# A fused attention and matrix-product kernel: whole loads of two first tiles, and the small products of tiles 3 to 5 placed in other bursts

## The chip, the core and the metric

The kernel runs on one core of a Trainium2 chip. Five engines work from queues of their own: TensorE (PE, with its weight loads as PEld), VectorE (DVE), ScalarE (ACT), GpSimd (POOL) and SyncE (SP), which here only issues the DMAs. The metric is the device time of one execution in microseconds, median of three. The profile is of one further execution.

## What is computed

```python
def sm_attn(qq, kk, vv):                 # per batch (8) and head (8), head_dim 64
    s = scale * qq @ kk.T
    a = exp(s - max(s));  a = a / (sum(a) + 1e-9)
    return a @ vv
p_packed = sm_attn(p, k, v)              # 32 packed queries over 576 keys
out      = sm_attn(q, p_packed, p_packed) # 576 queries over the 32 packed ones
x = out as (4608 tokens, 512)
h = max(x @ w1, x @ w2, x @ w3)          # 768 wide
result = h @ w_out
```

## The kernel before

A batch is 576 tokens, worked in two halves of 288 columns. Heads are packed four to a tile: `r` (0, 1) is the parity of a head in its pair. Per batch PE does, in the program's names:

- `s1`: the first scores (`scores`, stage S), 16 small products of 64 rows by 32 columns of the array (form 64*32). Their softmax weights `a1` come from DVE (maximum) and ACT (exponential), stage A.
- `spread` (stage X): DVE transposes `a1` in blocks into `x`, one DMA writes it to DRAM (`xk`), four DMAs read it back turned (`xt`).
- `av` (`values`, stage V): 40 products of `xt` with `v`, then (stage K) a transpose, which gives `pt`, the packed values.
- `s2` (`queries`, stage Q): the second scores, 16 products of 64*32, and their softmax (stage B), which gives `a2h` and `a2l`, high and low part.
- `pw` (`project`, stage P): for each of six tiles j of the 768 hidden features, 8 products of `pt` with the weights `w`, 64*32. ACT and DVE read them out of PSUM into `ph` and `pl`.
- `mi` (`layer_in`, stage N): 216 full products (128*128, 288 columns), in groups of six: one group is one tile j, one half, one of w1 to w3. A group's sum stands in a PSUM buffer of the pool `moe`, which has 4; it is free for the next group when ACT or DVE has taken it out (`maximum`, stage E).
- `mo` (`layer_out`, stage O): 126 full products with w_out, read out in stage F.

Small products stand in bursts between the full ones, since they use the array in another shape. PSUM has a second pool, `big`, with 2 buffers, for `s1`, `av`, `s2` and the tiles of `pw` that `project` doesn't put into `moe`.

The order of everything is written out by hand: START (batches 0 and 1 and the conversion of the weights), then LOOP once for each batch b = 2 to 7. Each word is one step of a stage; `P03` is tile 3 of batch b, `P10` tile 0 of batch b+1, `V101` is `av` of batch b+1, `Q1` its `s2`, `X1` its spread. A letter v, g or a behind a word says which engine does the step. Each engine runs its part of that order in the order in which it stands; it only waits for what an instruction needs. DMAs are issued by SP in the same way. Each DMA issue takes one of eight completion counters in turn, so it also waits until the DMA eight before it has landed. `J` words are products of no use that fill time at the start.

Of the kernel before, what the change touches and what calls it, by code (L numbers as in the profile page):

```python
# [20 lines left out]
B, H, S, D, NP = 8, 8, 576, 64, 32  # L21
# [24 lines left out]


START = """
k00 k01 J10 S0 A01 A01 J7 A01 A00 A00 v01 w00 C00 q010 v00 q000 A01 A00 A00v C00 C00 J1 V00 Z00 q001 V00 V01 Z01
V01 J1 K0 w01 K0v C01 J1 Q0 B010 B010 q011 J1 Q0 C01 k11 k10 C01 B001 B001 B000 B011 B000 B011 w02 B000v B011v  # L50
C00 k21 B010 C01 B010 B010 B000 B000 B000v J11 S1 B011 k20 w12 C02 C02 J12 S2 B001 A10 B001 C02 C02 P00 B010v
A11 A10 A11 B011 B010 B011 C12 B000 P00 B010g Z10 C12 B011 B010 w11 B010v B000g B000 v10 B001 A21 B001v P00 P00
J8 A11 Z11 B001 A20 B001g B011g B000v w10 v11 B000v A21 J1 A10 B001 q10 C12 B001v A20 C10 N00 w21 B011 B010v A10
A11 V101 C10 B011 P00 N00 V101 C11 C11 B001v C11 C12 E000 q11 N00 C21 K1 C21 w20 N00 C10 K1v J1 Q1 E000 E000 C20
C20 C21 w22 Z20 B011 N00 w30 B10 C22 C11 C10 J2 P01 P01 N00 E001 w31 B11 B11 C21 C20 C20 C22 C22 C22 w50 C30 P01
w32 B10 C31 C30 P10 w41 X2 B10v J6 N01 E010 C30 N01 C31 P02 P02 C31 w40 C32 N01 E001 E010 E001 C30 N01 N01 E011
C32 B11 C31 P02 C32 C32 E010 N02 v21 E011 N02 v20 N02 N02 w42 w52 B10 X2 H00 E020 E020 E020 B11 B11 B11v C40 C40
C40 C40 C41 C41 P03 N02 C41 P03 E021v P03 N01 N02 E021 w51 C42 C42 N03 N03 B10 X2 C41 B11 C52 B10 P10 w64 E011
C50 N03 C42 C42 E030v P10 H00 B10 Z21 N03 C52 P04 B11g P11 P04 E031 E021 E030 P04 N03 B10g w62 C52 N03 E030 N04
N04 E031 B11 C51 C51 B10 E040 E031 C52 E040 w65 H00 C50 B11 B11v P11 C51 N04 N04 B10 B10v N04 N04 E041 C64 C64  # L60
E041 E041 E040 C51 N10 C62 H02v E100 N10 N10 C50 C50 V201 q20 P11 P05 H03v w63 H02 C65 C65 C65 N11 E110 C64 C64
H03v C65 N11 N10 E100 V201 K2 E110 P05 C62 W2 N10 P05 E100 E101v C62 w60 H02v C63 N11 E110 H03v K2 q21 Q2 B21
N05 N05 C63 C63 B20 H01 E050 C63 N10 B20 B20 C60 P13 E050 W2 E101 C60 E101 P12 P13 W2 N05 H04v N05 P13 E050 C62
N11 E111 C60 N11 E111 B20 N11 W1v H03v P12 W1 P12 N13 E111 E051 N05 E051 H04 N05 N12 E051 C60 E130 N13 W1 N13
N12 W2 W2v P15 w61 C61 C61 C61 E120v E120 E130 P14 W1 W1v N13 C61 W0v W0v N12 E120 N12 W2 N13 H05g N12 W2 W2 P15
E130 H03 N12 E131 P15 B21 E121 E121 E131 P14 P14 N15 N15 N15 W0 N13 E150 E150 N14 N14 W2 N14 N14 N15 N15 E121
H03v H05 W2 W0 W0v E131 N14 W1 E150 E140 E140 E140 W0 W0 W0 H13 H04v H05 B20 E151v B20 O0 N14 E141v E141 E151
W1v N15 H01v E141 W0 k30 O0 F0 H10 O0 F0 O0 O0 O0 E151 H05v H10 W1 k31 P20 B20 H01 F0 H01v F0 W0v H10v P21 H05
B21v F0 H01 H05v P22 H01v F0 H12 H11 H14v O0 W1g H11v O0 H11v P21 B21 F0 O0 O0 H13 P20 P20 P20 H11v F0 H12 H12v
B20 O0 F0 F0 F0 F0 H13 W1v P20 O0 B20 O0 O0 H14 F0 H14v F0 F0 B21 O1 F0 H15 H15v H15 O1 H11 B21 H13v F1 F1 H15v  # L70
H15 H13v P22 O1 F1 H11v O1 H13v H15v O1 B20 F1 O1 O1 B20 O1 F1 B21 B21g P21 O1 O1 F1 F1 F1 F1 F1 F1 F1 P22 B21
O1 F1 O1 O1 F1 B21 B21 F1 O1 F1
"""


LOOP = """
S1 A10 N02 N02 N02 N02 A11 N02 E020v A10 E020 E020 N00 N00 E021v E000 Z10 X1 E021 N02 A11 P03 X1 P05 E021 H02v
P03 P04 N01 N00 v11 N00 v10 P03 P03 P03 E001 q10 N03 N03 N00 N00 H02g E000 N03 N03 N03 E030v E030 E010 N01 Z11
N03 E000 E001 E001 H00v H00 H02v E031v P04 q11 E030 H00 N01 E031 E031 P04 E010 E010 N01 N01 N01 E011 E011 E011
X1 V101 V101 H03g H03 N04 N04 N04 N04 P05 k20 K1 E041 N04 H03v N04 H01g H01v H01v K1 Q1 E040v H01 H01 H03 H03  # L80
P05 E040 E041 E040 E041 B11 B11 N05 N05 N05 N05 B10 E050 E050 H04 B10 E050 N05 B11 H04 H04 E051 E051 N05 E051
P10 B11 B10 P11 P12 H05 H05 B11 H05v P10 O0 O0 P10 O0 B10 B10 B11v H05v P12 P11 F0 B10v P10 O0 F0 H01v H03v
H05 O0 O0 F0 H05 B11 F0 P12 B10 k21 B10g O0 O0 O0 F0 P11 F0 F0 O0 B10 F0 B11g B11 F0 F0 B10g B10v P10 B11g F0
F0 O0 O0 O0 F0 F0 B11v O0 F0 F0
"""


# [1 line left out]
def fused_kernel(ctx: ExitStack, tc: tile.TileContext, kp, qt, va, vb, wi, wo, out):  # L89
# [48 lines left out]
    def doze(n):  # L138

        for i in range(0, n, 4):  # L140
            k = min(n - i, 4)
            ps = ps_moe.tile([P, 512], F32, name=f"idle{len(dozes)}", tag="moe")
            dozes.append(ps)
            nc.tensor.matmul(  # L144
                out=ps[:, 0:k * P], lhsT=ident, rhs=ident.unsqueeze(1).to_broadcast([P, k, P]),
                start=True, stop=True,
            )
# [280 lines left out]
    def project(b, j):  # L428

        parts = [slice(0, R)]  # L430
        if j == 0 and b != 1 or j == 3 and b >= 2:

            parts = [slice(r, r + 1) for r in range(R)]
            ps = [ps_moe.tile([P, 512], F32, name=f"pw{b}_{j}_{r}", tag="moe") for r in range(R)]
            src = [x[:, 0:NW * P].unsqueeze(1) for x in ps]
        else:
            x = ps_big.tile([P, R, 512], F32, name=f"pw{b}_{j}", tag="big")
            ps, src = [x[:, r] for r in range(R)], [x[:, :, 0:NW * P]]
        for n in range(4):
            for r in range(R):  # L440
                o = slice(64 * r, 64 * r + 64)
                nc.tensor.matmul(  # L442
                    out=ps[r][NP * n:NP * n + NP, 0:NW * P],
                    lhsT=pt_sb[b % 2][o, NP * n:NP * n + NP],
                    rhs=w_sb[o, j, n * NW * P:(n + 1) * NW * P],
                    start=True, stop=True,
                )
        yield 1
        hi = pool.tile([P, R, NW * P], F32R, name=f"ph{b}_{j}", tag="ph", bufs=3)
        lo = pool.tile([P, R, NW * P], F32R, name=f"pl{b}_{j}", tag="pl", bufs=3)  # L450
        pw[b, j] = (hi, lo)
        for r, x in zip(parts, src):
            nc.scalar.activation(out=hi[:, r], in_=x, func=AF.Copy, scale=2.0 ** -WS)  # L453
            yield 1
            nc.vector.scalar_tensor_tensor(  # L455
                out=lo[:, r], in0=x, scalar=2.0 ** -WS, in1=hi[:, r].bitcast(F32), op0=ALU.mult, op1=ALU.subtract,
            )
            yield 1
# [148 lines left out]
    def weigh_and_turn(b, r):  # L607
# [5 lines left out]
    stages = {  # L613
        "S": scores, "A": weigh_and_turn, "Z": invert, "X": spread, "V": lambda b, *rs: values(b, rs), "K": packed, "Q": queries,
        "B": attend, "C": convert, "P": project, "N": layer_in, "E": maximum, "H": halves,
        "O": layer_out, "F": finish, "W": weights,
    }
# [3 lines left out]
    def run(words, base):  # L621

        for word in words.split():
            name = word.rstrip("vga")
            chosen[0] = word[len(name):] or None
            kind, x = name[0], [int(i) for i in name[1:]]
            if kind == "J":
                doze(int(name[1:]))
                continue
            if kind not in "wCW":  # L630
                x[0] += base
                if x[0] >= B:
                    continue
            if kind in loads:
                loads[kind](*x)
            else:
                key = (kind, *x)
                if key not in begun:
                    begun[key] = stages[kind](*x)
                next(begun[key], None)  # L640
        chosen[0] = None

    with tc.manual_schedule():
        run(START, 0)
        for b in range(2, B):
            run(LOOP, b)


# [41 lines left out]
```

## Time and profile before

| | us |
|---|---|
| median of 3 | 468.36 (468.21 to 468.43) |
| the profiled execution | 468.03 |
| its span | 466.2 |
| PE busy | 457.3 (98%) |
| DVE, ACT, POOL busy | 349.8, 172.6, 207.1 |
| one batch of the loop, from one `s1` to the next | 54.2 |

The span is what the profiler sees from the first to the last instruction; 1.8 us of the execution's own time lie around it. PE is busy nearly always, so what counts is what PE's busy time is made of, and the few places where it waits.

### The profile page before, as it was taken

To read this page: it belongs to the slowest core of one execution; us is meant where nothing else is said; L and a number is where in the kernel's file an instruction comes from. 1 tells how busy PE (TensorE), PEld (TensorE's weight loads), DVE (VectorE), ACT (ScalarE), POOL (GpSimd) and SP (SyncE) were. 2 spreads that over 40 slices of the span, in tenths; PEclk is the share of its full clock that TensorE was granted. 3 is DMA by queue.
4 is the path that set the end of the run, shared out by engine and by line. 5 is a ranking of instruction groups with operands and counts; after the bars stand their busy time and mean duration, and the time that the engine had idled before them with its cause. 6 is when DMAs were issued, how large, how long until landed. Compare 5 with 4: busy or idle time off the path is not lost.

```text
span 466.2 us, 11503 instructions
## 1 busy us (share of the span) xinstructions
PE 457.3 (98%) x4728; PEld 405.3 (87%) x4728; DVE 349.8 (75%) x763; ACT 172.6 (37%) x333; POOL 207.1 (44%) x180
## 2 busy tenths in 40 slices
PE   8899999999999999999999999999999999999996
PEld 3456987998998998989899898989989898998996
DVE  1799989999887677766888678786777678865652
ACT  3486975744332236022340226122350324402330
POOL 0357766756332156503653055612565036531542
PEclk9999999999999999999999999999999999999999
DMA  8999883011127510193104820075101820020002
GB/s 301 403 381 312 315 296 130 1 58 56 57 73 247 192 58 1 49 308 108 59 27 141 257 100 1 27 250 188 59 1 62 296 52 1 27 76 1 2 4 99
DMA packets 25540, 59.20 MB, mean 127 GB/s; under 512 B 2448, under 2 KB 15760, under 8 KB 25488
## 3 DMA queue, kind: packets, MB, share of 16 engines
q1 hardware_dynamic: 25488, 58.47, 36.7%
q8 instruction: 37, 0.61, 0.5%
q14 instruction: 15, 0.12, 0.1%
HBM read 45.48 MB, written 12.98 MB: 125 GB/s over the span
## 4 chain that ended last, share of the span: by engine, by line
PE 92%; DVE 4%; DMA 2%; ACT 0%; issue 0%; POOL 0%; POOLq 0%; ACTq 0%
PE mi L477 49%; PE mo L546 29%; PE pw L442 7%; DMA kt<-in_kp 2%; PE s L253 2%; PE av L342 2%; PE s L370 1%; PE idle L144 1%; DVE mx L266 1%; DVE xt L219 0%; DVE w_sb L203 0%; DVE r L491 0%; ACT a L271 0%; PE tp L342 0%; DVE xl L136 0%
## 5 line engine op out<-in xcount | busy, mean ns | idle before, releaser
L477 PE MATMUL mi<-a2h,ph 128*128 128x288 f32 x576 | 173.9, 302 | 0.7 <-ACT r L131 0.5
L477 PE MATMUL mi<-a2l,ph 128*128 128x288 f32 x576 | 169.7, 295 | 0.0
L477 PE MATMUL mi<-a2h,pl 128*128 128x288 f32 x576 | 169.7, 295 | 0.0
L477 PEld LDWEIGHTS mi<-a2h,ph 128*128 128x128 f32 x576 | 108.1, 188 | 15.5 <-issue 7.1
L477 PEld LDWEIGHTS mi<-a2h,pl 128*128 128x128 f32 x576 | 108.1, 188 | 0.0
L477 PEld LDWEIGHTS mi<-a2l,ph 128*128 128x128 f32 x576 | 108.1, 188 | 0.0
L491 DVE TENSOR_TENSOR r<-mi,r 128x288 f32<-128x288 f32 x192 | 83.3, 449 | 32.6 <-PE mi L477 30.2
L131 ACT COPY r<-mi 128x288 f32<-128x288 f32 x60 | 23.4, 401 | 122.8 <-PE mi L477 122.7
L455 DVE SCALAR_TENSOR_TENSOR pl<-pw,ph 128x768 fp32r<-128x768 f32 (+1 forms) x61 | 46.8, 775 | 4.5 <-ACT ph L453 3.6
L453 ACT ACTIVATE ph<-pw 128x768 fp32r<-128x768 f32 (+1 forms) x61 | 39.9, 675 | 18.8 <-PE pw L442 15.1
L546 PE MATMUL mo<-ych,xl 128*128 128x288 f32 x144 | 42.5, 295 | 0.0
L546 PE MATMUL mo<-ych,xh 128*128 128x288 f32 x144 | 42.4, 295 | 0.0
L546 PE MATMUL mo<-ycl,xh 128*128 128x288 f32 x144 | 42.4, 294 | 0.0
L136 POOL TENSOR_TENSOR yal<-r,yah 128x576 fp32r<-128x576 f32 x13 | 18.6, 1430 | 46.1 <-ACT yah L131 46.1
L271 ACT ACTIVATE a<-s,nm 128x576 f32<-128x576 f32 x16 | 11.9, 741 | 66.8 <-DVE nm L267 60.1
L442 PE MATMUL pw<-w_sb,pt 64*32 64x384 f32 x768 | 36.0, 487 | 0.3 <-POOL w_sb L207 0.3
L207 POOL TENSOR_TENSOR w_sb<-w_sb,wi 128x512 int32<-128x512 int32 x18 | 24.2, 1349 | 26.7 <-DVE z L282 11.8
L515 POOL TENSOR_TENSOR r<-r 128x288 f32<-128x288 f32 (+1 forms) x25 | 27.9, 1128 | 17.5 <-issue 9.0
L133 POOL CAST yah<-r 128x576 fp32r<-128x576 f32 x6 | 4.0, 662 | 57.0 <-DVE r L515 57.0
L546 PE MATMUL mo<-yah,xh 128*128 128x288 f32 x96 | 28.8, 300 | 0.0
L133 DVE COPY r<-mi 128x288 f32<-128x288 f32 x36 | 16.3, 455 | 16.2 <-PE mi L477 16.2
L546 PE MATMUL mo<-ybh,xl 128*128 128x288 f32 x96 | 28.3, 295 | 0.0
(117 smaller groups left out, 885.2 us busy)
## 6 DMA issues: line engine op xcount, KB each, us to landing
kt<-in_kp SPq DMA_DIRECT2D x16, 640.0 KB, 5.2
wi<-in_wi SPq DMA_DIRECT2D x18, 512.0 KB, 6.9
v<-in_va SPq DMA_DIRECT2D x16, 512.0 KB, 5.9
q<-in_qt SPq DMA_DIRECT2D x14, 576.0 KB, 7.1
xk<-x SPq DMA_DIRECT2D x6, 576.0 KB, 4.9
wi<-in_wo SPq DMA_DIRECT2D x6, 512.0 KB, 5.0
out_t<-r SPq DMA_DIRECT2D x8, 288.0 KB, 2.2
out_t<-t SPq DMA_DIRECT2D x8, 288.0 KB, 2.3
```

Source lines behind the costliest of these rows:

```text
L131: e.copy(out=out, in_=src)
L133: e.tensor_copy(out=out, in_=src)
L136: on(default).tensor_tensor(out=lo, in0=src, in1=hi.bitcast(F32), op=ALU.subtract)
L207: nc.gpsimd.tensor_tensor(out=dst.bitcast(I32), in0=dst.bitcast(I32), in1=up, op=ALU.add)
L271: nc.scalar.activation(out=a.rearrange("p (a b) -> p a b", a=2), in_=s[:, :, 0:HS], func=AF.Exp, bias=nm, scale=SCALE, accum_out=z,)
L442: nc.tensor.matmul(out=ps[r][NP * n:NP * n + NP, 0:NW * P], lhsT=pt_sb[b % 2][o, NP * n:NP * n + NP], rhs=w_sb[o, j, n * NW * P:(n + 1) * ...
L453: nc.scalar.activation(out=hi[:, r], in_=x, func=AF.Copy, scale=2.0 ** -WS)
L455: nc.vector.scalar_tensor_tensor(out=lo[:, r], in0=x, scalar=2.0 ** -WS, in1=hi[:, r].bitcast(F32), op0=ALU.mult, op1=ALU.subtract,)
L477: nc.tensor.matmul(out=sums[b, j, hf, x][:, 0:HS], lhsT=w[:, r, x * P:(x + 1) * P], rhs=a[:, c], start=(r == 0 and n == 0), stop=(r == R - ...
L491: nc.vector.tensor_tensor(out=h, in0=sums[b, j, hf, i][:, 0:HS], in1=h, op=ALU.max)
L515: less = lambda out, x, y: on("g").tensor_tensor(out=out, in0=x, in1=y, op=ALU.subtract)
L546: nc.tensor.matmul(out=ps[:, 0:HS], lhsT=w[:, x, m * P:(m + 1) * P], rhs=h[:, z], start=(p == 0 and i == 0), stop=(p == NQ - 1 and i == 2),)
```

## The change

Two edits. In START the first batch's two `q` tiles are each loaded whole instead of in two halves; whole means 128 rows of 4608 B, a half 256 pieces of 1152 B. LOOP gets a new order for batches 2 to 5, and the old one, now called LAST, stays for batches 6 and 7. `project` puts tile 5 of batches 2 to 5 into the pool `moe` instead of `big`.

```diff
 START = """
-k00 k01 J10 S0 A01 A01 J7 A01 A00 A00 v01 w00 C00 q010 v00 q000 A01 A00 A00v C00 C00 J1 V00 Z00 q001 V00 V01 Z01
-V01 J1 K0 w01 K0v C01 J1 Q0 B010 B010 q011 J1 Q0 C01 k11 k10 ...
+k00 k01 J10 S0 A01 A01 J7 A01 A00 A00 v01 w00 C00 q01 v00 q00 A01 A00 A00v C00 C00 J1 V00 Z00 V00 V01 Z01 V01 J1
+K0 w01 K0v C01 J1 Q0 B010 B010 J1 Q0 C01 k11 k10 ...
 LOOP = """
-S1 A10 N02 N02 N02 N02 A11 N02 E020v A10 E020 E020 N00 N00 E021v E000 Z10 X1 E021 N02 A11 P03 X1 P05 E021 H02v
...
+S1 N02 v11 A10 N00 E020a N01 A10 N01 N00 N02 A11 N01 N00 v10 E010 N00 N02 E010 E000 N00 A11 N01 N02 X1 X1 E020
...
+N01 N02 N02 E001 N00 E021a E000 E000 X1 E010 P03 Z11 Z10 E020 E001 E011 E011 P03 E021 P04 V101 N01 P03 E001 P04
...
+LAST = """
+(the old LOOP)
@@ project
-        if j == 0 and b != 1 or j == 3 and b >= 2:
+        if j == 0 and b != 1 or j == 3 and b >= 2 or j == 5 and 2 <= b < B - 2:
@@
-            run(LOOP, b)
+            run(LOOP if b < B - 2 else LAST, b)
```

SP's first DMAs, at the start of the program. Before:

```order
L154 DMA wi0_0_137<-in_wi 128x512
L175 DMA q1_140<-in_qt 128x2x288
L166 DMA v0_142<-in_va 128x1024
L167 DMA v0_142<-in_vb 64x256
L175 DMA q0_145<-in_qt 128x2x288 x2
L154 DMA wi0_1_217<-in_wi 128x512
L175 DMA q1_140<-in_qt 128x2x288
L160 DMA kt3_249<-in_kp 128x1280
```

The same place with the change:

```order
L166 DMA wi0_0_137<-in_wi 128x512
L187 DMA q1_140<-in_qt 128x1152
L178 DMA v0_142<-in_va 128x1024
L179 DMA v0_142<-in_vb 64x256
L187 DMA q0_145<-in_qt 128x1152
L166 DMA wi0_1_216<-in_wi 128x512
L172 DMA kt3_247<-in_kp 128x1280
```

The second half of `q1` now goes ahead of `v0` and of all that follows; the bytes up to `kt3` are the same.

PE in batch 3, from the last full product ahead of `pw` to `av`. Before, the three tiles are one burst, and `av` stands 96 full products later, alone:

```order
L477 MATMUL mi3_2_1_2_2899<-a2l3_1_2790,ph3_2_2633 128x288
L442 MATMUL pw3_3_0_2909<-w_sb_74,pt1_76 32x384
...
L442 MATMUL pw3_5_2923<-w_sb_74,pt1_76 32x384 x8
L442 MATMUL pw3_4_2937<-w_sb_74,pt1_76 32x384 x8
L477 MATMUL mi3_1_0_0_2946<-a2h3_0_2747,ph3_1_2636 128x288
...
L342 MATMUL av4_3111<-v8_2970,xt4_3106 32x64 x2
...
L477 MATMUL mi3_4_0_0_3159<-a2h3_0_2747,ph3_4_3060 128x288
```

With the change:

```order
L489 MATMUL mi3_0_1_2_2973<-a2l3_1_2804,ph3_0_2541 128x288
L454 MATMUL pw3_3_0_2991<-w_sb_74,pt1_76 32x384
...
L454 MATMUL pw3_4_3015<-w_sb_74,pt1_76 32x384 x8
L354 MATMUL av4_3024<-v8_2896,xt4_2985 32x64 x2
...
L489 MATMUL mi3_1_1_2_3065<-a2h3_0_2780,ph3_1_2536 128x288
...
L382 MATMUL s2_4_1_3124<-q9_3079,pt0_75 32x288 x4
L454 MATMUL pw3_5_0_3137<-w_sb_74,pt1_76 32x384
...
L489 MATMUL mi3_4_0_0_3150<-a2h3_0_2780,ph3_4_3074 128x288
```

`av` follows `pw` of tiles 3 and 4 directly, and tile 5 follows `s2`. Between `s1` and `pw` there are now 102 full products (48 before). On SP the write `xk` and the four reads `xt` now stand ahead of the next batch's two loads of `q`, which stood ahead of `xk` before.

DVE at the start of batch 3's full products, from the maxima of `s1` (`nm`) to the block transposes `x`. Before:

```order
L267 TENSOR_SCALAR nm4_1_2856<-mx4_1_2855 128x1
L133 COPY r3_1_2866<-mi3_2_0_0_2827 128x288
L491 TENSOR_TENSOR r3_1_2866<-mi3_2_0_1_2834,r3_1_2866 128x288
L491 TENSOR_TENSOR r3_1_2866<-mi3_2_0_2_2841,r3_1_2866 128x288
L133 COPY r3_1_2866<-mi3_2_1_0_2848 128x288
...
L315 STREAM_TRANSPOSE x4_2893<-a1_4_0_2868 128x5x32 x2
L315 STREAM_TRANSPOSE x4_2893<-a1_4_0_2868 128x4x32 x2
L491 TENSOR_TENSOR r3_1_2866<-mi3_2_1_1_2859,r3_1_2866 128x288
L315 STREAM_TRANSPOSE x4_2893<-a1_4_1_2906 128x5x32 x2
```

With the change:

```order
L279 TENSOR_SCALAR nm4_1_2879<-mx4_1_2878 128x1
L503 TENSOR_TENSOR r3_0_2899<-mi3_1_0_1_2857,r3_0_2899 128x288
L327 STREAM_TRANSPOSE x4_2941<-a1_4_0_2854 128x5x32 x2
L327 STREAM_TRANSPOSE x4_2941<-a1_4_0_2854 128x4x32 x2
L327 STREAM_TRANSPOSE x4_2941<-a1_4_1_2924 128x5x32 x2
L327 STREAM_TRANSPOSE x4_2941<-a1_4_1_2924 128x4x32 x2
L503 TENSOR_TENSOR r3_1_2845<-mi3_2_0_1_2871,r3_1_2845 128x288
```

One operation that reads a sum (`mi3_1_0_1`, the fourth group of six) now stands ahead of the transposes instead of four, and nothing stands between the two sets; other readings of sums have moved to ACT.

## Rows read from the trace of the kernel before

**Rows 1.** The page: busy time by engine, and the engines' shares in the chain that ended last.

```profile
PE 457.3 (98%) x4728; PEld 405.3 (87%) x4728; DVE 349.8 (75%) x763; ACT 172.6 (37%) x333; POOL 207.1 (44%) x180
...
PE 92%; DVE 4%; DMA 2%; ACT 0%; issue 0%; POOL 0%; POOLq 0%; ACTq 0%
```

**Rows 2.** Busy time of PE, PEld, DVE, ACT and POOL in one batch of the loop (with the number of instructions), the granted clock, DMA's share and GB/s.

```profile
197.23:251.44 54.21, 54.21 (x592) 49.32 (x598) 40.73 (x92) 16.15 (x32) 22.53 (x19) 1.00 0.35 113
```

**Rows 3.** The chain that ended last, in batch 3 of the loop: start, us, engine, tile, line, number of instructions (each small product counts twice).

```profile
204.90 2.10 PE pw L442 x48
207.00 12.93 PE mi L477 x96
219.93 1.39 PE av L342 x80
...
226.37 1.13 PE s L370 x32
```

**Rows 4.** The same chain in START: bursts of one and of two tiles of `pw`, and `av` with one tile of `pw` behind it, up to the full products that follow.

```profile
45.30 0.81 PE pw L442 x16
...
58.44 1.45 PE pw L442 x32
...
68.83 1.31 PE av L342 x73
...
70.86 2.58 PE mi L477 x18
```

**Rows 5.** PE in order of time, the last products of that `av` (start, us, form).

```profile
69.93 0.22 PE L342 MATMUL av<-v,xt 64*32 64x64 f32 x2
```

**Rows 6.** PE in order of time, at both ends of batch 3's `av`.

```profile
219.64 0.29 PE L477 MATMUL mi<-a2l,ph 128*128 128x288 f32 x1
219.86 1.46 PE L342 MATMUL av<-v,xt 128*32 128x64 f32 x80
221.25 0.40 PE L477 MATMUL mi<-a2h,ph 128*128 128x288 f32 x1
221.48 0.29 PE L477 MATMUL mi<-a2h,pl 128*128 128x288 f32 x1
```

**Rows 7.** DVE in order of time, batch 0, with the idle time ahead of an instruction and who ended it.

```profile
11.91 0.27 DVE L133 COPY a1t<-pa 64x128 f32<-64x128 f32 x1
...
15.99 0.48 DVE L393 STREAM_TRANSPOSE e<-s 128x288 f32<-128x288 f32 x1 [0.88 <-PE s L370]
...
21.76 0.76 DVE L266 TENSOR_REDUCE mx<-s 128x1 f32<-128x576 f32 x1 [0.45 <-PE s L253]
```

**Rows 8.** PE in order of time, batch 0: the products with `v`, the last filler products, the first scores of batch 1.

```profile
12.24 1.73 PE L342 MATMUL pa<-v,a1t 128*32 128x64 f32 x80
...
16.88 2.63 PE L144 MATMUL idle<-ident 128*128 128x512 f32 x6
20.37 1.32 PE L253 MATMUL s<-kt 64*32 64x288 f32 x32 [0.86 <-DMA kt<-in_kp]
```

**Rows 9.** DMA in the first 50 us: GB/s in slices of 1.25 us; SP's issue of `v0`; its time from issue to landing.

```profile
GB/s 0 147 315 426 396 391 322 365 349 294 409 396 441 385 403 423 413 414 405 411 398 320 403 367 333 375 408 418 406 397 354 295 305 387 223 315 154 315 392 283
...
4.18 0.62 SPq L166 DMA_DIRECT2D v<-in_va  x1
...
v<-in_va SPq DMA_DIRECT2D x1, 512.0 KB, 7.9
```

**Rows 10.** DVE in order of time, batch 3: the reading of the fourth group of six, and the first set of transposes.

```profile
201.76 0.46 DVE L133 COPY r<-mi 128x288 f32<-128x288 f32 x1
202.14 0.14 DVE L282 TENSOR_SCALAR z<-z 128x1 f32<-128x1 f32 x1
...
202.40 0.95 DVE L315 STREAM_TRANSPOSE x<-a 128x160 f32<-128x160 f32 x4
203.28 0.41 DVE L491 TENSOR_TENSOR r<-mi,r 128x288 f32<-128x288 f32 x1
```

**Rows 11.** SP in order of time: the write `xk` and the four reads `xt` of batch 3, and of batch 4.

```profile
205.50 0.33 SPq L318 DMA_DIRECT2D xk<-x  x1
210.76 1.75 SPq L322 DMA_DIRECT2D xt<-xk  x4
...
259.73 0.33 SPq L318 DMA_DIRECT2D xk<-x  x1
263.80 1.75 SPq L322 DMA_DIRECT2D xt<-xk  x4
```

**Rows 12.** From issue to landing, us (last number): the last read `xt` of batch 4, with a load right behind it; the last two of batch 6, with none; a store of 288 KB with nothing ahead of it.

```profile
xt<-xk SPq DMA_DIRECT2D x1, 128.0 KB, 4.9
...
xt<-xk SPq DMA_DIRECT2D x2, 128.0 KB, 3.3
...
out_t<-r SPq DMA_DIRECT2D x1, 288.0 KB, 2.2
```

**Rows 13.** DVE in order of time: a low part `yal`, two transposes of second scores, a maximum over them.

```profile
213.66 0.75 DVE L136 TENSOR_TENSOR yal<-r,yah 128x576 fp32r<-128x576 f32 x1
...
228.80 0.84 DVE L393 STREAM_TRANSPOSE e<-s 128x288 f32<-128x288 f32 x2
...
229.90 0.73 DVE L397 TENSOR_REDUCE m<-e 128x18 f32<-128x576 f32 x1
```

More of the change, by code (lines that the diff above doesn't have):

```diff
@@ L48 @@
 START = """
-k00 k01 J10 S0 A01 A01 J7 A01 A00 A00 v01 w00 C00 q010 v00 q000 A01 A00 A00v C00 C00 J1 V00 Z00 q001 V00 V01 Z01
[L50 to L72, printed above, removed]
+k00 k01 J10 S0 A01 A01 J7 A01 A00 A00 v01 w00 C00 q01 v00 q00 A01 A00 A00v C00 C00 J1 V00 Z00 V00 V01 Z01 V01 J1
+K0 w01 K0v C01 J1 Q0 B010 B010 J1 Q0 C01 k11 k10 C01 B001 B001 B000 B011 B000 B011 w02 B000v B011v C00 k21 B010
@@ new lines @@
+C01 B010 B010 B000 B000 B000v J11 S1 B011 k20 w12 C02 C02 J12 S2 B001 A10 B001 C02 C02 P00 B010v A11 A10 A11
+B011 B010 B011 C12 B000 P00 B010g Z10 C12 B011 B010 w11 B010v B000g B000 v10 B001 A21 B001v P00 P00 J8 A11 Z11
+B001 A20 B001g B011g B000v w10 v11 B000v A21 J1 A10 B001 q10 C12 B001v A20 C10 N00 w21 B011 B010v A10 A11 V101
+C10 B011 P00 N00 V101 C11 C11 B001v C11 C12 E000 q11 N00 C21 K1 C21 w20 N00 C10 K1v J1 Q1 E000 E000 C20 C20 C21
+w22 Z20 B011 N00 w30 B10 C22 C11 C10 J2 P01 P01 N00 E001 w31 B11 B11 C21 C20 C20 C22 C22 C22 w50 C30 P01 w32 B10
@@ new lines @@
+C31 C30 P10 w41 X2 B10v J6 N01 E010 C30 N01 C31 P02 P02 C31 w40 C32 N01 E001 E010 E001 C30 N01 N01 E011 C32 B11
+C31 P02 C32 C32 E010 N02 v21 E011 N02 v20 N02 N02 w42 w52 B10 X2 H00 E020 E020 E020 B11 B11 B11v C40 C40 C40 C40
+C41 C41 P03 N02 C41 P03 E021v P03 N01 N02 E021 w51 C42 C42 N03 N03 B10 X2 C41 B11 C52 B10 P10 w64 E011 C50 N03
+C42 C42 E030v P10 H00 B10 Z21 N03 C52 P04 B11g P11 P04 E031 E021 E030 P04 N03 B10g w62 C52 N03 E030 N04 N04 E031
+B11 C51 C51 B10 E040 E031 C52 E040 w65 H00 C50 B11 B11v P11 C51 N04 N04 B10 B10v N04 N04 E041 C64 C64 E041 E041
@@ new lines @@
+E040 C51 N10 C62 H02v E100 N10 N10 C50 C50 V201 q20 P11 P05 H03v w63 H02 C65 C65 C65 N11 E110 C64 C64 H03v C65
+N11 N10 E100 V201 K2 E110 P05 C62 W2 N10 P05 E100 E101v C62 w60 H02v C63 N11 E110 H03v K2 q21 Q2 B21 N05 N05 C63
+C63 B20 H01 E050 C63 N10 B20 B20 C60 P13 E050 W2 E101 C60 E101 P12 P13 W2 N05 H04v N05 P13 E050 C62 N11 E111 C60
+N11 E111 B20 N11 W1v H03v P12 W1 P12 N13 E111 E051 N05 E051 H04 N05 N12 E051 C60 E130 N13 W1 N13 N12 W2 W2v P15
+w61 C61 C61 C61 E120v E120 E130 P14 W1 W1v N13 C61 W0v W0v N12 E120 N12 W2 N13 H05g N12 W2 W2 P15 E130 H03 N12
@@ new lines @@
+E131 P15 B21 E121 E121 E131 P14 P14 N15 N15 N15 W0 N13 E150 E150 N14 N14 W2 N14 N14 N15 N15 E121 H03v H05 W2 W0
+W0v E131 N14 W1 E150 E140 E140 E140 W0 W0 W0 H13 H04v H05 B20 E151v B20 O0 N14 E141v E141 E151 W1v N15 H01v E141
+W0 k30 O0 F0 H10 O0 F0 O0 O0 O0 E151 H05v H10 W1 k31 P20 B20 H01 F0 H01v F0 W0v H10v P21 H05 B21v F0 H01 H05v
+P22 H01v F0 H12 H11 H14v O0 W1g H11v O0 H11v P21 B21 F0 O0 O0 H13 P20 P20 P20 H11v F0 H12 H12v B20 O0 F0 F0 F0
+F0 H13 W1v P20 O0 B20 O0 O0 H14 F0 H14v F0 F0 B21 O1 F0 H15 H15v H15 O1 H11 B21 H13v F1 F1 H15v H15 H13v P22 O1
@@ L73 @@
+F1 H11v O1 H13v H15v O1 B20 F1 O1 O1 B20 O1 F1 B21 B21g P21 O1 O1 F1 F1 F1 F1 F1 F1 F1 P22 B21 O1 F1 O1 O1 F1
+B21 B21 F1 O1 F1
 """
 LOOP = """
+S1 N02 v11 A10 N00 E020a N01 A10 N01 N00 N02 A11 N01 N00 v10 E010 N00 N02 E010 E000 N00 A11 N01 N02 X1 X1 E020
+N01 N02 N02 E001 N00 E021a E000 E000 X1 E010 P03 Z11 Z10 E020 E001 E011 E011 P03 E021 P04 V101 N01 P03 E001 P04
+P03 E021 q11 V101 K1 P03 H02g q10 N03 K1 P04 E030a H00g E011 N03 N03 Q1 H00g H01v P05 E030 H01g N04 N03 E040a
+P05 N03 k20 E030 N04 B10 N03 H02v N04 B10 E031a P05 E040 P05 E031 H02g E031 P05 H03a N04 E040 H00v N05 B11 B11
@@ L77 @@
+B10 B10 N04 H01g E041v B11 E041 N04 E041 P10 P12 E050 H04v P11 B11 P11 H04 P10 H03 B10 B11 N05 H01 N05 E050 H03g
+H04 E050 N05 B10a N05 E051v P12 E051 P10 N05 O0 E051 H03 B11a O0 H01 H01v O0 H03v H05 H05v F0 F0 O0 O0 F0 H05v
+H05v H03v B10 F0 H05 O0 H05v O0 B11 O0 O0 F0 P12 F0 B10g F0 O0 B11v O0 F0 F0 B11 F0 B10 O0 F0 k21 F0 O0 P10 B10a
+B11a B10g P11 F0 F0 O0 F0 P10 F0 B11g
+"""
+LAST = """
 S1 A10 N02 N02 N02 N02 A11 N02 E020v A10 E020 E020 N00 N00 E021v E000 Z10 X1 E021 N02 A11 P03 X1 P05 E021 H02v
@@ L81 @@
 P05 E040 E041 E040 E041 B11 B11 N05 N05 N05 N05 B10 E050 E050 H04 B10 E050 N05 B11 H04 H04 E051 E051 N05 E051
-P10 B11 B10 P11 P12 H05 H05 B11 H05v P10 O0 O0 P10 O0 B10 B10 B11v H05v P12 P11 F0 B10v P10 O0 F0 H01v H03v
-H05 O0 O0 F0 H05 B11 F0 P12 B10 k21 B10g O0 O0 O0 F0 P11 F0 F0 O0 B10 F0 B11g B11 F0 F0 B10g B10v P10 B11g F0
-F0 O0 O0 O0 F0 F0 B11v O0 F0 F0
+P10 B11 B10 P11 P12 H05 H05 B11 H05v P10 O0 O0 P10 O0 B10 B10 B11v H05v P12 P11 F0 B10v P10 O0 F0 H01v H03v H05
+O0 O0 F0 H05 B11 F0 P12 B10 k21 B10g O0 O0 O0 F0 P11 F0 F0 O0 B10 F0 B11g B11 F0 F0 B10g B10v P10 B11g F0 F0 O0
+O0 O0 F0 F0 B11v O0 F0 F0
 """
```

## The prediction

> **What bounds the kernel now.** I read the page first: PE is busy 457.3 of 466.2 us and has 92% of the chain that ended last; DVE, the next engine, has 75% of the span [rows 1]. Next one batch of the loop by itself: in its 54.21 us DVE is busy 40.73, POOL 22.53, ACT 16.15, DMA 0.35 of the time, and the granted clock is 1.00, so TensorE's upper level, 2.4 GHz [rows 2]. Nothing but PE can be the bound there as long as the others come in time. The chain then gives PE's own pieces in batch 3, and they touch one another: 48 products `pw`, 96 `mi`, the 80 of `av`, later `s2` [rows 3]. So in the loop time comes only from PE's pieces getting shorter, and is lost only where PE has to wait for something that it didn't wait for. START is different: DVE and DMA are in its chain too, so I read it engine by engine in order of time [rows 7, 8, 9].
>
> **Part 1, the bursts of batches 2 to 5.** The change makes three bursts (`pw` of three tiles; `av`; `s2`) into two (`pw` of two tiles with `av`; `s2` with one tile of `pw`). The number of products is the same.
>
> - A burst of one tile of `pw` takes 0.81, of two 1.45, of three 2.10 [rows 3, 4]: each tile 0.645, and 0.165 for coming in. `av` takes 1.39, `s2` 1.13 [rows 3].
> - A boundary between full products and a burst costs something besides. The last full product and `av` start 0.22 apart, and the first and second full product behind it 0.23 [rows 6], where full products are 12.93 / 96 = 0.135 apart [rows 3]. That is 0.09 + 0.10 = 0.19 for a burst.
> - Before: 2.10 + 1.39 + 1.13 + 3 x 0.19 = 5.19 us. After, if `av` behind `pw` costs what it costs alone: (1.45 + 1.39) + (1.13 + 0.645) + 2 x 0.19 = 5.00. Saved: 0.195 a batch, 0.78 in four.
> - START has the two side by side, in the other order: from `av` at 68.83 to the full products at 70.86 are 2.03 [rows 4], which is 1.39 + 0.64. There the coming-in was free. If it is free here too, the saving is 0.36 a batch and 1.44 in all.
>
> Between 0.78 and 1.44 I take 0.78. In START the last products of `av` have the form 64*32 [rows 5], which is that of the `pw` behind them, so that seam changes no shape; with the change `pw`'s 64*32 meets the first products of `av`, 128*32 [rows 6]. The seam between `s2` and `pw` is 64*32 on both sides, and there I take the 0.645 without coming-in.
>
> The Trainium skill (TensorEngine Tiling (Array Packing), section Tiling Modes) says that a change of tiling mode, and not just of the tile, drains TensorE. By it the seam from `pw` to `av` isn't free, and the sum stays at -0.78; by START's row it would be -1.44. No row here has this very seam.
>
> **Part 2, `av`'s data.** `av` now stands 102 full products behind `s1`, with 16 of `pw` ahead of it; before it was 48 + 96 products and 24 of `pw`. So the way of `a1` through DRAM must be done some 4 us sooner. I count both sides from the moment when DVE begins to read the fourth group of six, since the change puts the transposes right behind that.
>
> The data: 0.38 for the reading (201.76 to 202.14), 0.88 for the first set of transposes (202.40 to 203.28), 0.95 for the second [rows 10]: `xk` is issued at 2.2. From its issue to that of the first `xt` it was 5.26 in one batch and 4.07 in the next, with two loads of `q` queued ahead of it on SP [rows 11]. These now come behind. A store of 288 KB with nothing ahead takes 2.2 [rows 12]; the bytes of a busy stream, 295 KB at about 405 GB/s [rows 9], add 0.73: 2.9. Between 2.9 and 4.1 I take 3.4, since some load is generally under way. The fourth `xt` is issued 1.3 behind the first (the four take 1.75 [rows 11], of which three intervals count), and lands 3.3 (no load behind) to 4.9 (a load behind) later [rows 12]; I take 4.3, as the `q` loads now do come behind. In all 2.2 + 3.4 + 1.3 + 4.3 = 11.2, and with the ends 9.7 to 12.5.
>
> PE: of the 102 products 24 are done when the fourth group is. 78 x 0.135 = 10.5, a boundary 0.09, `pw` 1.45 [rows 3, 4, 6], less 0.1 by which DVE begins behind PE's end (`s1` ends at 20.37 + 1.32, `mx` begins at 21.76 [rows 7, 8]): 11.9. So the data are there 0.7 ahead. At the worst PE waits 0.6 in each batch, at the best there are 2 to spare. I take no wait. Before, the 96 extra products hid this way; now 0.7 us do, and any delay of DVE at the transposes comes out of it.
>
> **Part 3, PSUM.** Tile 5 now takes a buffer of `moe`, and the readings of sums are dealt out anew between DVE and ACT. One place is tight: the buffer for the next batch's `pw` of tile 0. It is free when DVE has done a maximum over sums 0.41 [rows 10], a low part 0.75, two transposes of second scores 0.84, a maximum 0.73 [rows 13] and a copy 0.46 [rows 10], 3.2 with 0.1 for its beginning; PE wants it four groups later, 24 x 0.135 + 0.09 = 3.3. A tie: 0 to 0.4 of wait, I take 0.05 a batch, 0.2 in all. Behind that `pw` on PE stand the rest of the burst and all full products, so such a wait is paid whole. DVE as a whole has 54.2 - 40.7 = 13.5 us of a batch free [rows 2], and ACT still more, so neither becomes the bound by what is moved to it.
>
> **Part 4, START.** The two `q` tiles are 1.18 MB. While their halves (in pieces of 1152 B) pass, the stream runs at 322, 365, 349 and 294 GB/s, mean 332; around it at about 405 [rows 9]. At 405 they need 0.64 less (3.55 to 2.91), and what comes behind is earlier by that: the keys which end PE's idle 0.86 ahead of batch 1's `s1` at 20.37 [rows 8] would be there at about 19.6.
>
> But the second half of `q1`, 295 KB, now goes ahead of `v0`: 0.73 later, less some 0.15 by which the first half passes sooner. `v0` lands at 4.18 + 7.9 = 12.08 [rows 9], and now at about 12.6. PE's products with `v` begin at 12.24, then released by DVE's copy, which ends at 12.18 [rows 7, 8]; they would begin at about 12.7, 0.45 later. DVE's work from 15.99 on hangs on that and moves by 0.45; but DVE was idle 0.45 at 21.76, waiting for `s1` [rows 7]. PE's filler products end at 16.88 + 2.63 = 19.51 [rows 8] and now at 19.96; `s1` follows and ends at 21.3, so `mx` begins at about 21.8 as before. The 0.45 that the keys give and the 0.45 that `v0` takes cancel. Bounds: -0.45 (if `v0` isn't late) and +0.3 (if `v0` loses all of the 0.73, and nothing else of it is made up); I take +0.05.
>
> **The sum.** -0.78 + 0.2 + 0.05 = -0.53. The profiled execution took 468.03, of which 466.2 is span; the median of the runs is 0.33 above it. Taken off the median: 468.36 - 0.53 = 467.8 us. 0.2% is 0.94 us, about what a measurement of this kernel can tell from no change; so this is "same": faster begins below 467.42 and slower above 469.30.
>
> **The rivals.**
>
> - *`av` waits for its data.* For it: `xk` to `xt` of 5.26 in batch 3 [rows 11], where I take 3.4, and 4.9 for a read with a load behind it, as there now is. Against it: both were measured with more traffic ahead. Its price is each microsecond beyond 0.7 in the way of the data, four times over. From a wait of 0.2 a batch the gain of the bursts is gone, from 0.37 the kernel is slower by 0.2%. With 0.5 a batch: 467.8 + 2.0 = 469.8, slower. Chance 0.20.
> - *`v0` isn't late in START.* If the second half of `q1` passes beside the loads ahead of `v0` and not in front of it, only the earlier keys remain, and DVE's idle 0.45 goes: -0.78 + 0.2 - 0.45 = -1.03, 467.3, faster. For it: the slices before 7.5 us already run at about 390 [rows 9], so more requests may only fill gaps. Against it: one queue, served in its order. Chance 0.14.
> - *The seam from `pw` to `av` is free*, as in START: -1.44 + 0.25 = -1.19, 467.2, faster. For it 2.03 us in a row [rows 4], against it the forms [rows 5, 6]. Chance 0.10.
> - *DVE is late at tile 0's buffer*, by 0.35 a batch: 467.8 + 1.2 = 469.0, still within 0.2%. It speaks for it that two numbers of 3.2 and 3.3 meet; against it that DVE has time to spare on the whole. Chance 0.06.
>
> The forecast keeps 0.50, with a range of its own of 467.3 to 468.5 (Part 4's -0.45 at one end; at the other Part 3 with 0.2 a batch). Faster: the second and third rival and a sliver of the forecast, 0.25. Slower: the first, 0.20. Same: the rest, 0.55. The range reaches from half way past the two faster cases to the slower one: 466.9 to 469.8.
>
> **What the trace after would show.** Part 1: `pw` of 32 and `av` of 80 records in one piece of the chain, 2.84 long (2.67 if the seam is free), `s2` with one tile 1.78, and a batch of 54.0 instead of 54.2. Part 2: no idle PE ahead of `av`, the last `xt` landed up to 1 us earlier; a wait of `av` for DMA `xt` makes the first rival true. Part 3: PE waits for DVE ahead of the first `pw` of tile 0 of no more than 0.1 to 0.2. Part 4: slices from 7.5 to 12.5 us near 400 GB/s, the products with `v` at about 12.7, `s1` at about 20.0 and `mx` still at about 21.8. The prediction is wrong if PE waits in the loop anywhere else, above all behind `s1`, where the readings of sums have changed engines, or if DVE reaches the transposes late.

## The result

The changed kernel takes 470.82 us (median of 5 runs, 470.43 to 471.19) and the kernel before, on the same chip, 468.26: a ratio of 1.0059, 95% interval 1.0048 to 1.0070. It is 0.6% slower, 2.6 us, where 467.8 was forecast; 1.0 us outside the range.

The page of after: busy time by engine, then the engines' shares in the chain that ended last.

```profile
PE 458.5 (98%) x4728; PEld 407.4 (87%) x4728; DVE 345.9 (74%) x747; ACT 180.3 (38%) x361; POOL 205.8 (44%) x176
...
PE 83%; DVE 12%; DMA 2%; issue 1%; SPq 1%; ACT 0%; POOL 0%; DVEq 0%
```

DVE as a whole is busy less than before (345.9 against 349.8 [rows 1]), and yet its share in the chain went from 4% to 12%. One batch of the loop, by windows (length; busy time of PE, PEld, DVE, ACT, POOL; clock, DMA share, GB/s):

```profile
198.18:253.08 54.90, 54.54 (x592) 49.95 (x598) 39.74 (x87) 18.07 (x39) 22.17 (x19) 1.00 0.34 111
```

It is 54.90 where it was 54.21 [rows 2], at the same clock of 1.00. The profiled execution's span grew by 3.0 us, 466.2 to 469.2: from batch 2's first scores to batch 6's it is 219.64 (143.28 to 362.92) where it was 216.90 (142.99 to 359.89), so the four batches give 2.74, about 0.69 each; the other 0.29 is START, where the first scores of batch 2 begin at 143.28 instead of 142.99. The chain in batch 3 says where in the batch (start, us, engine, tile, line, count):

```profile
213.03 1.45 PE pw L454 x32
214.48 1.39 PE av L354 x80
...
219.33 1.13 PE s L382 x32
...
224.52 0.83 DVE r L503 x2
...
227.40 0.77 DVE e L405 x2
228.19 0.75 DVE m L409
...
230.47 1.45 DVE r L527
231.92 1.32 DVE z L416 x2
...
233.66 2.67 PE mi L489 x18
```

The two bursts are as forecast. But from 224.5 on the chain runs through DVE for 9 us, and in that row of work one instruction is out of size: a subtraction `r L527` of 288 columns takes 1.45 us. Its own size is 0.45: DVE does a subtraction of the same form in that time elsewhere in the same batch, where POOL does nothing:

```profile
240.34 0.45 DVE L527 TENSOR_TENSOR r<-r 128x288 f32<-128x288 f32 x1
```

PE in order of time shows what the long one costs:

```profile
229.21 2.31 PE L454 MATMUL pw<-w_sb,pt 64*32 64x384 f32 x48
231.46 0.40 PE L489 MATMUL mi<-a2h,ph 128*128 128x288 f32 x1
...
233.01 0.29 PE L489 MATMUL mi<-a2l,ph 128*128 128x288 f32 x1
233.66 0.40 PE L489 MATMUL mi<-a2h,ph 128*128 128x288 f32 x1 [0.36 <-DVE r L503]
233.90 0.29 PE L489 MATMUL mi<-a2h,pl 128*128 128x288 f32 x1
```

Two products that should start 0.13 apart start 0.65 apart, and the one behind comes 0.24 later instead of 0.13, as it does behind a burst (0.23 in [rows 6]). So the wait costs 0.52 + 0.10 = 0.62 us, although the view puts only 0.36 down as idle time: products overlap, and a product's row ends after the next could have begun. A second, smaller sign is in the burst: it lasts 2.25 us to the next full product, 231.46 - 229.21, where three tiles took 2.10 [rows 3]. No view shows a wait there. Its second product starts behind DVE's copy (228.86 to 229.31), which by the order of the program frees tile 0's buffer, so 0.14 is put down to that; without this copy on DVE the burst is 2.10 again (below, E041 on ACT).

So 0.62 + 0.14, less 0.07 for the bursts (below), give the 0.69 of a batch.

DVE and POOL in after, in order of time, around the long subtraction:

```profile
228.86 0.45 DVE L145 COPY r<-mi 128x288 f32<-128x288 f32 x1
229.41 1.02 DVE L503 TENSOR_TENSOR r<-mi,r 128x288 f32<-128x288 f32 x2
230.47 1.45 DVE L527 TENSOR_TENSOR r<-r 128x288 f32<-128x288 f32 x1
231.84 1.40 DVE L416 TENSOR_REDUCE z<-e 128x18 f32<-128x576 f32 x2
233.16 1.01 DVE L503 TENSOR_TENSOR r<-mi,r 128x288 f32<-128x288 f32 x2
```

```profile
230.19 1.40 POOL L148 TENSOR_TENSOR ybl<-r,ybh 128x576 fp32r<-128x576 f32 x1
231.56 2.40 POOL L527 TENSOR_TENSOR r<-r 128x576 f32<-128x576 f32 x2
```

DVE's subtraction begins at 230.47 while POOL's subtraction `ybl` runs (230.19 to 231.59), and ends at 231.92, 0.33 behind POOL's end. The two sums `z` behind it take 1.40 together beside the next instruction of POOL, no more than in the runs below. The word for the long one is `H04v`: the change took this subtraction of tile 4 from POOL (0.80 us there, at 226.95 in batch 3 of before) and gave it to DVE. The kernel before has a case of the same kind in every batch, at a place where nothing waits for it (DVE, then POOL):

```profile
249.48 1.79 DVE L136 TENSOR_TENSOR a2l<-et,a2h 128x576 fp32r<-128x576 f32 x1
```

```profile
249.22 1.43 POOL L594 TENSOR_TENSOR t<-v,t 128x576 f32<-128x576 f32 x1
```

Without company a low part of that size takes 0.75 [rows 13].

### The profile page after: what moved, and what is told of

Same layout as the page of the kernel before. It is cut to its first block, busy times and chain, and to the rows that moved or that the text cites. A ratio compares the mean times of both kernels' runs of the same rounds, so it can differ in the third digit from the quotient of the medians.

```text
span 469.2 us, 11492 instructions
## 1 busy us (share of the span) xinstructions
PE 458.5 (98%) x4728; PEld 407.4 (87%) x4728; DVE 345.9 (74%) x747; ACT 180.3 (38%) x361; POOL 205.8 (44%) x176
## 4 chain that ended last, share of the span: by engine, by line
PE 83%; DVE 12%; DMA 2%; issue 1%; SPq 1%; ACT 0%; POOL 0%; DVEq 0%
PE mi L489 44%; PE mo L558 29%; PE pw L454 5%; DVE r L503 3%; DMA v<-in_va 2%; PE av L354 2%; PE s L382 2%; DVE z L416 1%; DVE e L405 1%; DVE r L527 1%; PE s L265 1%; DVE m L409 1%; DVE yal L148 1%; DVE mx L278 1%; DVE pl L467 0%
## 5 line engine op out<-in xcount | busy, mean ns | idle before, releaser
L527 POOL TENSOR_TENSOR r<-r 128x288 f32<-128x288 f32 (+1 forms) x37 | 38.3, 1048 | 84.7 <-DVE r L503 49.4
L143 ACT COPY r<-mi 128x288 f32<-128x288 f32 x72 | 27.8, 401 | 118.5 <-PE mi L489 118.4
L467 DVE SCALAR_TENSOR_TENSOR pl<-pw,ph 128x384 fp32r<-128x384 f32 (+1 forms) x65 | 47.4, 737 | 17.4 <-ACT ph L465 17.1
L465 ACT ACTIVATE ph<-pw 128x384 fp32r<-128x384 f32 (+1 forms) x65 | 41.0, 644 | 42.1 <-PE pw L454 27.1
L454 PE MATMUL pw<-w_sb,pt 64*32 64x384 f32 x768 | 37.7, 487 | 0.3 <-POOL w_sb L219 0.3
L558 PE MATMUL mo<-ybl,xh 128*128 128x288 f32 x96 | 28.3, 295 | 0.0
L558 PE MATMUL mo<-yal,xh 128*128 128x288 f32 x96 | 28.3, 295 | 0.0
L558 PE MATMUL mo<-yah,xl 128*128 128x288 f32 x96 | 28.3, 295 | 0.0
L558 PE MATMUL mo<-ybh,xh 128*128 128x288 f32 x96 | 28.3, 295 | 0.0
```

The costliest lines, as they stand in the source:

```text
L143: e.copy(out=out, in_=src)
L454: nc.tensor.matmul(out=ps[r][NP * n:NP * n + NP, 0:NW * P], lhsT=pt_sb[b % 2][o, NP * n:NP * n + NP], rhs=w_sb[o, j, n * NW * P:(n + 1) * ...
L467: nc.vector.scalar_tensor_tensor(out=lo[:, r], in0=x, scalar=2.0 ** -WS, in1=hi[:, r].bitcast(F32), op0=ALU.mult, op1=ALU.subtract,)
L527: less = lambda out, x, y: on("g").tensor_tensor(out=out, in0=x, in1=y, op=ALU.subtract)
L558: nc.tensor.matmul(out=ps[:, 0:HS], lhsT=w[:, x, m * P:(m + 1) * P], rhs=h[:, z], start=(p == 0 and i == 0), stop=(p == NQ - 1 and i == 2),)
```

## Theories and experiments

**Theory 1**: a DVE instruction with both inputs in SBUF stands still while POOL's runs; the 1.0 us that the subtraction loses makes DVE late with the readings of tile 5's sums, and PE waits. No data tie the two: by the program `ybl` comes from the pair of tiles 2 and 3, the subtraction works on tile 4. The Trainium skill (SBUF — State Buffer, section Who interferes with whom) says just that: such an instruction contends with a GpSimd instruction that reads SBUF, and whichever starts first holds the shared pair of ports for its whole length. By it the reductions `z` are free of that; the rows agree on both, with 1.45 instead of 0.45 for the subtraction and no change for `z`. The runs show durations only; that it is ports which the two engines share is the page's statement. **Rivals**: DVE simply has too much in a row there, and each microsecond taken off counts as one; or the new order of the bursts itself costs the time.

### H04 on POOL

Of the order only the words around the edit are shown, here and below.

```diff
-E041 P10 P12 E050 H04v P11 B11 P11 H04
+E041 P10 P12 E050 H04 P11 B11 P11 H04
```

> The whole change, but the word H04v in LOOP becomes H04: the subtraction of two half tiles (r<-r, 128x288) of tile 4 goes from DVE to POOL. Theory 1 (DVE's subtraction, with both inputs in SBUF, stands still while POOL's ybl runs: 1.45 us instead of 0.45): all of PE's wait behind the pw of tiles 0 to 2 goes, 0.62 a batch, so 2.5 us less than the whole change, a batch of 54.3. Rival (DVE just has 9 us of work in a row there, and what is taken off shortens the wait one for one): only its own 0.45 goes, a wait of 0.17 a batch stays, 1.8 us less, a batch of 54.45. Rival 2 (the new order of the bursts costs it): no change, 54.9.

468.69 us (11 runs), 2.1 less than the change and 1.0013 of before (1.0005 to 1.0022). The time alone decides nothing: theory 1 expected 2.5 less, the first rival 1.8. The batches tell more; the last three of the four, by windows:

```profile
196.99:251.31 54.32, 54.32 (x592) 49.98 (x599) 38.37 (x86) 18.07 (x39) 22.78 (x20) 1.00 0.35 112
251.31:305.61 54.30, 54.30 (x591) 49.95 (x599) 38.37 (x86) 18.08 (x39) 22.49 (x20) 1.00 0.34 112
305.61:360.15 54.54, 54.54 (x591) 50.00 (x598) 38.37 (x86) 18.08 (x39) 23.07 (x20) 1.00 0.36 113
```

Two of them are at 54.30 to 54.32 (and so is the first, 142.69 to 196.99), as theory 1 said, and not 54.45; PE's idle time behind `pw` is gone. The 0.14 is still there, since DVE's copy hasn't moved:

```profile
228.02 2.31 PE L454 MATMUL pw<-w_sb,pt 64*32 64x384 f32 x48
...
230.26 0.40 PE L489 MATMUL mi<-a2h,ph 128*128 128x288 f32 x1
```

The last batch of the four has 0.24 more: right behind its `s1`, at 307.30, two full products start 0.26 apart. The weight load of the second one waits there for POOL, for the low part `a2l`:

```profile
307.55 0.19 PEld L489 LDWEIGHTS mi<-a2l,ph 128*128 128x128 f32 x1 [0.19 <-POOL a2l L148]
```

That is a part of what is missing from the 2.5; why POOL comes later to `a2l` in this batch is open.

### E041 on ACT

```diff
-B10 B10 N04 H01g E041v B11 E041
+B10 B10 N04 H01g E041 B11 E041
```

> The whole change, but the word E041v becomes E041: the copy of the first sum of tile 4, second half (0.38 us on DVE), goes to ACT; the subtraction H04v stays on DVE. Theory 1: DVE comes to the subtraction 0.38 sooner, at about 0.1 ahead of POOL's ybl instead of 0.28 behind its start, so the subtraction takes 0.45 instead of 1.45 and POOL's ybl becomes longer; PE's wait of 0.62 goes, and so does the 0.14 for which the second product of pw waits for that copy: 3.0 us less than the whole change, a batch of 54.15. Rival (DVE is simply full): 0.38 off the wait and the 0.14: 2.1 us less, a batch of 54.4, the subtraction still at 1.45.

467.79 us (11 runs), 3.0 less than the change, as expected; 0.9994 of before (0.9986 to 1.0003). A batch, and in it DVE and POOL:

```profile
196.96:251.11 54.15, 54.15 (x591) 49.40 (x598) 38.57 (x86) 18.37 (x40) 22.18 (x19) 1.00 0.35 113
```

```profile
228.68 0.65 DVE L527 TENSOR_TENSOR r<-r 128x288 f32<-128x288 f32 x1
229.25 1.40 DVE L416 TENSOR_REDUCE z<-e 128x18 f32<-128x576 f32 x2
231.18 0.46 DVE L503 TENSOR_TENSOR r<-mi,r 128x288 f32<-128x288 f32 x1 [0.53 <-PE mi L489]
```

```profile
227.85 1.16 POOL L411 TENSOR_TENSOR e<-e,m 128x576 f32<-128x576 f32 x1 [0.79 <-PE mi L489]
228.96 1.64 POOL L148 TENSOR_TENSOR ybl<-r,ybh 128x576 fp32r<-128x576 f32 x1
```

0.38 us less work ahead of it, and the subtraction is 0.80 shorter: it is now the first in line, behind POOL's `e` (which ends at 229.01; 0.32 later the subtraction is done), and `ybl` is the one that is held, 1.64 instead of 1.40. DVE has 0.53 idle where it was late. The rival's 54.4 is out. The expected 0.45 was too little: the subtraction ends 0.32 behind POOL's `e`, which the expectation overlooked.

### The same work, one place later

On top of E041 on ACT. Where the subtraction went ahead of the two sums `z`, it now goes between them:

```diff
-E050 H04v P11 B11 P11 H04 P10 H03 B10 B11
+E050 P11 B11 P11 P10 H03 B10 H04v H04 B11
```

> The kernel of e041_act with DVE's subtraction H04v put one instruction later, behind the first of the two sums z (0.74 us) instead of ahead of it (the cast that reads it goes with it on ACT); DVE's work is the same. Theory 1: the subtraction now begins at about 0.4 behind the start of POOL's ybl instead of 0.3 ahead of it, so it takes 1.3 us instead of 0.65 and ybl 1.42 instead of 1.64; DVE comes to the next reading of a sum about 0.7 later, of which 0.5 was idle time, so PE is held 0.1 to 0.3 us in a batch: 54.25 to 54.45, 0.4 to 1.2 us more than e041_act. Rival (DVE's load decides, not who runs beside it): the subtraction at 0.45 to 0.65 in its new place, a batch of 54.15, no difference.

468.37 us (11 runs), 0.6 more than without it; four batches of 0.11 more make 0.45 of that. The batch, DVE and POOL:

```profile
197.53:251.79 54.26, 54.26 (x591) 49.42 (x598) 39.25 (x86) 18.36 (x40) 22.16 (x19) 1.00 0.36 112
```

```profile
229.14 0.74 DVE L416 TENSOR_REDUCE z<-e 128x18 f32<-128x576 f32 x1
229.80 1.48 DVE L527 TENSOR_TENSOR r<-r 128x288 f32<-128x288 f32 x1
231.20 0.74 DVE L416 TENSOR_REDUCE z<-e 128x18 f32<-128x576 f32 x1
```

```profile
229.54 1.42 POOL L148 TENSOR_TENSOR ybl<-r,ybh 128x576 fp32r<-128x576 f32 x1
```

Same instructions, 1.48 us instead of 0.65, and `ybl` back at 1.42. PE pays for it at the same place as with the change, though less, since DVE had 0.53 to spare there (0.15 and 0.24 between starts, where 0.13 is usual):

```profile
232.21 0.29 PE L489 MATMUL mi<-a2l,ph 128*128 128x288 f32 x1
232.36 0.40 PE L489 MATMUL mi<-a2h,ph 128*128 128x288 f32 x1
232.60 0.30 PE L489 MATMUL mi<-a2h,pl 128*128 128x288 f32 x1
```

DVE's load didn't change; who began first did. This rules out the rival that only the load counts.

### The two edits apart

> The kernel before with the new START alone. If the trace of after is right about START (v0 there 0.84 us later, the products with v at 13.08 instead of 12.24, 0.45 of it swallowed by DVE's idle time ahead of mx): +0.3 us against before, mx of batch 1 at about 22.1. If the forecast's sizes were right and after's v0 was late by chance: within 0.1 us of before, the products with v at about 12.7 and mx at 21.8.

> The changed LOOP and project with the old START. If the two edits simply add up: 0.3 us less than the whole change, so +2.3 to +2.7 us against before, with a batch of 54.9 us. If the late START pushes the loop's waits about (the batch's period changes with it): a batch of clearly less or more than 54.9.

The new START alone (the diff's first part): 468.27 us (12 runs), 0.1 more than before, ratio 1.0011 (1.0000 to 1.0022); 0.3 were expected, though the profiled execution has `mx` at 22.20, near the 22.1 that went with them. The new LOOP with the old START: 471.02 us (5 runs), 2.9 more, 1.0063 (1.0051 to 1.0075), a batch of 54.92. So nearly all of the slowdown is the loop's, and that the edits touch one another can't be seen in these times.

Of START the profiled execution shows (PE, then DVE):

```profile
13.21 1.73 PE L342 MATMUL pa<-v,a1t 128*32 128x64 f32 x80 [1.39 <-DMA v<-in_va]
```

```profile
22.20 0.75 DVE L266 TENSOR_REDUCE mx<-s 128x1 f32<-128x576 f32 x1
```

The products with `v`, and what hangs on them, in ten profiled executions, in us:

| START | the rest | products with `v` begin | `mx` of batch 1 begins |
|---|---|---|---|
| old | kernel before | 12.24 | 21.76 |
| old | LOOP as changed | 12.35 | 21.61 |
| old | LOOP with E041 on ACT | 12.38 | 21.37 |
| new | LOOP as changed | 13.08 | 22.08 |
| new | kernel before | 13.21 | 22.20 |
| new | LOOP with H04 on POOL | 12.53 | 21.52 |
| new | LOOP with E041 on ACT | 12.62 | 21.61 |
| new | the same, H04 between the two `z` | 13.03 | 22.03 |
| `v0` first | kernel before | 12.39 | 21.38 |
| `v0` first | LOOP with E041 on ACT | 11.92 | 20.91 |

With the new START `mx` stands 8.99 or 9.00 behind the products with `v` in all five: the keys are always in time, and `v0` alone sets the end (in the table's last two rows, too, it is 8.99). With the old one it was 9.52, 9.26 and 8.99: there it depends on when the keys land. `v0` is late by 0.57 on the mean (12.89 against 12.32), with 0.7 between one execution and the next.

### v0 ahead of q1

```diff
-q01 v00 q00
+v00 q01 q00
```

> The kernel before with the new START (whole loads of q), but v0 issued ahead of q1. Theory: in START the keys come sooner by what whole loads save, and v0's place in the queue costs it again; with v0 in front the products with v begin at about 12.2 again (DVE's copy sets them), the keys' idle time ends at about 19.6 to 20, and mx of batch 1 begins at 21.3 to 21.5 instead of 21.76: 0.2 to 0.45 us less than before. Rival: q1 is now the late one, the second scores of batch 0 wait for it, and mx is at 21.8 to 22.2: within 0.1 us of before or 0.4 more.

> The changed LOOP with E041 on ACT, and the old START. If the loop's part is 54.15 a batch whatever START does: four times 0.07 less than before, 467.8 to 467.9 where before is 468.15, and the difference to the same LOOP with the new START is what START is worth, 0.0 to 0.3 us.

> The changed LOOP with E041 on ACT, whole loads of q, and v0 issued ahead of q1. If both gains are there and add up: 0.3 from the loop and 0.2 to 0.45 from START, 467.4 to 467.7 where before is 468.15. If q1 becomes the late one: 467.8 to 468.2.

With the LOOP of before: 467.70 us (11 runs), 0.9989 of before (0.9981 to 0.9998), 0.4 us less and just clear of the noise; `mx` at 21.38. The whole loads do pay, once `v0` doesn't stand behind the longer `q1`. The LOOP with E041 on ACT: 467.70 with the old START (467.8 to 467.9 were expected), so START as changed is worth at most about +0.1 against it (467.79), within the noise. With `v0` first 467.26 (11 runs), 0.9983 of before (0.9975 to 0.9992), 0.9 us less, where 0.5 to 0.75 was expected: both gains are there and add up, and `v0` first is worth 0.4 here again. This beats both kernels, by 0.2% against before. PE and DVE in its START:

```profile
11.92 1.73 PE L354 MATMUL pa<-v,a1t 128*32 128x64 f32 x80
```

```profile
20.91 0.75 DVE L278 TENSOR_REDUCE mx<-s 128x1 f32<-128x576 f32 x1
```

## Why the prediction was wrong

**Part 3 is the step that failed.** It looked for the one place where a reader frees a buffer just in time, and costed DVE ahead of that: "DVE as a whole has 54.2 - 40.7 = 13.5 us of a batch free", so nothing that was moved to it could count. What decided stands behind that buffer: the subtraction begins 1.2 us behind the copy that frees it, and PE stops 2.2 us behind the end of the burst. The term that was left out is a subtraction moved from POOL to DVE, right beside one of POOL's: 0.45 of work that took 1.45, with nine microseconds of DVE's work without a gap around it. The mean share of an engine says nothing of such a stretch. The order of the changed program had the row (a `r<-r` of tile 4 on DVE behind the readings), and the trace of before had the price, in a row of 1.79 for a low part that takes 0.75 alone. Four times 0.62 are 2.5 us, against 2.6 timed for the whole change and 2.9 for the loop alone; the forecast had this term at nothing.

**Tile 0's buffer** was the right place with too small a value: 0.14 a batch instead of 0.05, within the ends of 0 to 0.4. The fourth rival has it in the right direction, at under half its 0.35.

**Part 1** was right in its pieces: 1.45 + 1.39 = 2.84 for `pw` with `av`, and from `s2` at 219.33 to the full products at 221.10 it is 1.77 (forecast 1.78). The seam from `pw` to `av` isn't free; the choice of 0.78 over 1.44, for which the Trainium skill's rule on the tiling mode (TensorEngine Tiling (Array Packing), section Tiling Modes) stood, held, and the third rival is out. But the gain as a whole was smaller than 0.195: with no wait left (E041 on ACT) a batch is 54.15, 0.07 less than 54.22 (the mean of before's four). The saved boundary is partly given back, since the products of `mo` now follow `mi` directly (PE with E041 on ACT):

```profile
233.39 0.31 PE L489 MATMUL mi<-a2h,ph 128*128 128x288 f32 x1
233.55 0.30 PE L489 MATMUL mi<-a2h,pl 128*128 128x288 f32 x1
...
234.21 0.36 PE L558 MATMUL mo<-yah,xh 128*128 128x288 f32 x1
234.41 0.30 PE L558 MATMUL mo<-yah,xl 128*128 128x288 f32 x1
```

Before, a burst of `pw` stood between the two. The second `mo` now starts 0.20 behind the first instead of 0.13, and at three places a product is held 0.02 to 0.04 (here 0.16); what holds them is open. That is 0.13 in all, and 0.195 - 0.13 = 0.065.

**Part 2** was right: `av` never waits for its data. SP and the way to landing in after (last number: us):

```profile
204.97 0.33 SPq L330 DMA_DIRECT2D xk<-x  x1
207.79 2.73 SPq L334 DMA_DIRECT2D xt<-xk  x4
```

```profile
xt<-xk SPq DMA_DIRECT2D x2, 128.0 KB, 3.9
```

DVE begins to read the fourth group at 202.78; `xk` is issued 2.2 later (forecast 2.2), the first `xt` 2.8 behind it (3.4, and 2.9 as the lower end), the last about 1.3 later, at 209.1, and landed at 213.0. `av` begins at 214.4: 1.4 ahead, where 0.7 was forecast. With E041 on ACT the last `xt` is issued at 207.89 and takes 4.2, so it lands at 212.1, and `av` begins at 213.18, 1.1 behind. The first rival is out.

**Part 4** had the mechanism and nearly the size. The products with `v` were forecast 0.45 later and are 0.57 on the mean; DVE's idle 0.45 swallows that as far as it goes. +0.05 was forecast, +0.1 was timed, +0.29 is in this one profile, inside the bounds. What the forecast had as a rival, `v0` not late, is what `v0` first makes true: -0.4 us, where the rival said -0.45.

## What to carry to other kernels

Before giving an elementwise instruction to VectorE because it is the faster engine or has time to spare, look at what GpSimd does at that moment: a subtraction with both inputs in SBUF took as long here as GpSimd's instruction still ran, plus 0.32 or 0.33 us, and 0.4 us of work taken off ahead of it decided which of the two came first. Read an engine's slack from the stretch ahead of the wait in question, not from its share of a batch. A transfer that is made whole is also longer for what is queued behind it: put the one that is waited for first.

## What the runs showed that was not expected

- One instruction was 0.45 us alone, 0.65 and 1.45 to 1.48 with the same work around it, by how much of POOL's instruction was still to run when it began; in each of the stretched cases shown it ended 0.32 or 0.33 behind the end of POOL's.
- A wait of PE that the view puts at 0.36 idle cost 0.62: the next product starts 0.52 late, and the one behind it 0.10 more.
- Two executions with the same START differ by up to 0.7 us in when `v0` lands; on one profile alone +0.29 would have been taken for the edit's price.
